# Three of the expert slots of a fused attention and mixture kernel hold 64 tokens, six slots run before routing is complete

## The chip, the cores and the metric

The kernel runs on one core of one Trainium2 chip. The metric is the device time of one execution in microseconds (us). It was timed in three runs; one more execution was recorded by the hardware profiler. The engines are named as in the profile: PE is the matrix engine (PEld its loading of weights), DVE the vector engine, ACT the scalar engine, POOL the general engine, SP the engine that issues most DMA transfers.

## The reference: linear attention, a gated dense layer, then a top-1 mixture of eight experts

```python
x = attention(q, k, v, omega)               # 4 x 576 = 2304 tokens of 512 features
x = rmsnorm(x) * g
x = (silu(x @ w_gate) * (x @ w_val)) @ w_out          # 512 -> 1536 -> 512
# the mixture ("MoE 2"): eight experts, each token goes to one
logits = x @ w_gate2 + modality_bias[modality_id]
e_idx = argmax(logits, axis=1)
gate_w = softmax(logits)[arange(N), e_idx]
for e in range(8):
    mask = e_idx == e
    h = maximum(x[mask] @ w1[e], 0.0)       # 512 -> 1024
    out[mask] = gate_w[mask, None] * (h @ w2[e])      # 1024 -> 512
```

With the inputs of this case the reference sends 873, 291, 576 and 564 tokens to four experts and none to the other four. The expert of token 0 is the one with 873, and all of its tokens lie among the first 2048.

## The kernel before

Tokens lie in 18 tiles of 128. Attention and the dense layer run woven into each other, two tiles (a chunk) at a time; the hidden products are at L1156, the products back at L1226, the routing logits at L1292. Every 32-bit number that goes into a product is parted into a high and a low 16-bit half, and a product takes three matmuls (high by low, high by high, low by high).

The mixture works in **slots** of 128 tokens of one expert. `slots` (L1835) loads for a slot the four parts of the expert's parted weights (`load`, L1842: four DMAs of 1 MB from `split_dram`, issued by SP, L1852) into a place of a ring of `RING` = 3, and `compute` (L1886) does the work: POOL gathers the rows of the slot's tokens by an indirect DMA (L1892), PE transposes them (L1881), ACT and DVE part them (L307 and L313, L317), PE does the first product (L1916: 96 matmuls with the weights held in the engine and 128 tokens as columns), ACT takes the maximum with zero (L1933), the result is parted again, PE does the second product (L1945: 24 matmuls with the tokens held and 512 features as columns), ACT or DVE scales the rows (L850, L854), and POOL scatters them into the output (L1973).

Which tokens a slot holds comes from tables. The first `NEARLY` = 4 slots all belong to the expert of token 0 (padded where that expert has fewer tokens); their tables are made from the first 16 tiles while the dense layer still works on the last two (`early_picks` to `early_indices`), and they share one load of weights. The tables of all other slots are made when the last two tiles have their logits: the rank products on PE (L1591, L1595), then one after the other on DVE `counts` (L1704), `late_places`, `late_values` (L1733), `experts` (L1777), with the table products on PE (L1763) when `late_values` is done, and `late_indices`. `slot_i` (L1793) holds each slot's expert and the number of slots; SP waits for it before it can issue the loads of the slots after the early ones. The first `NFIXED` = 20 slots always run. Where more are needed, branches behind them run the rest (`further`, L1997); here 7 + 3 + 5 + 5 = 20 are needed.

The order of the work is written out beforehand by a planner (`Plan`, L71): every step has a cost, the engines that may do it, and a time at which it is wanted (`want`); the planner plays the steps through and fixes each engine's order and which engine does a step that several may do. `NUDGES` (L49) shifts the wanted times of chosen ranges of steps. `spare` (L485) sets 140 matmuls of no use into stretches in which the planner finds PE idle (L491).

## Time and profile before

| | |
|---|---|
| median of three runs | 834.04 us (829.54 to 836.36) |
| the profiled execution, its own time | 831.05 us |
| its span in the profile | 829.3 us |
| PE busy | 811.4 us, 98% of the span |
| DVE busy | 542.6 us, 65% |
| ACT busy | 478.3 us, 58% |
| POOL busy | 293.6 us, 35% |
| mean granted clock of PE | 0.995 |

An engine is busy while one of its instructions runs; a matmul's time in the profile reaches from its start to its modelled end, and matmuls overlap, so the distance of two starts tells the rate, not the length of one.

### The profile page before, as it was taken

Reading aid. Unit: us, or ns where it says so; the run is one execution under the profiler, and the core shown is the slowest. Engines: PE = TensorE matmul, PEld = TensorE weight load, DVE = VectorE, ACT = ScalarE, POOL = GpSimd, SP = SyncE. Lnnn points to the kernel's source line nnn. Section 1 sums busy time; section 2 is a strip of 40 time slices with the busy share of each in tenths; the row PEclk is TensorE's granted clock in tenths of the full one; section 3 lists DMA queues with packets and bytes.
Section 4 is the critical chain, followed back from the end, with each engine's and each line's share of the span. In section 5 each row is a group of like instructions: output and inputs, shape, how many; then the busy total and the mean of one; then the engine's idle time right before and its main releaser. Section 6 shows DMA issues by size and latency. Waiting matters only on the chain. (4 is left out here: it accounts for less than half of the span.)

```text
span 829.3 us, 19951 instructions
## 1 busy us (share of the span) xinstructions
PE 811.4 (98%) x7900; PEld 632.7 (76%) x7900; DVE 542.6 (65%) x1262; ACT 478.3 (58%) x1132; POOL 293.6 (35%) x425
## 2 busy tenths in 40 slices
PE   9999989999999999999999999999999999999995
PEld 8899878887656778887777777777777777777773
DVE  5788988997647888888889989777673111222220
ACT  4767667778525888767878877664333233223321
POOL 0288898574222224232314344222202111222211
PEclk9999999999999999999999999999999999999998
DMA  8525441337204578756677676855418999999980
GB/s 269 186 78 204 132 138 63 111 128 285 67 27 132 178 238 278 245 171 211 218 236 238 225 218 217 283 199 211 172 40 331 423 421 425 423 426 424 424 357 21
DMA packets 38579, 188.06 MB, mean 227 GB/s; under 512 B 5071, under 2 KB 5199, under 8 KB 21584
## 3 DMA queue, kind: packets, MB, share of 16 engines
q1 hardware_dynamic: 35280, 176.72, 59.1%
q0 software_dynamic: 3200, 10.01, 3.2%
q8 instruction: 64, 1.05, 0.5%
q14 instruction: 35, 0.29, 0.1%
HBM read 143.68 MB, written 43.55 MB: 226 GB/s over the span
## 5 line engine op out<-in xcount | busy, mean ns | idle before, releaser
L1156 PE MATMUL bank<-x,big 128*128 128x256 f16 x2592 | 310.7, 273 | 2.0 <-DVE plain L1180 1.6
L1156 PEld LDWEIGHTS <-big 128*128 128x128 f16 x2592 | 250.7, 98 | 49.4 <-issue 2.9
L1226 PE MATMUL bank<-big 128*128 128x512 f16 x648 | 160.2, 379 | 0.0
L317 POOL TENSOR_TENSOR big<-plain,big 128x256 f16<-128x256 f32 x101 | 80.2, 796 | 182.4 <-ACT big L307 143.6
L1916 PEld LDWEIGHTS <-big 128*128 128x128 f16 x1920 | 111.8, 98 | 12.0 <-issue 0.2
L1916 PE MATMUL bank<-plain,big 128*128 128x128 f16 x1920 | 116.4, 219 | 0.0
L1945 PE MATMUL bank<-big,plain 128*128 128x512 f16 x480 | 115.0, 379 | 0.0
L844 DVE SCALAR_TENSOR_TENSOR big<-big,e_fac 128x512 f16<-128x512 f32 x128 | 102.4, 806 | 8.2 <-ACT big L850 7.3
L1226 PEld LDWEIGHTS <-big 128*128 128x128 f16 x648 | 61.3, 99 | 49.6
L317 DVE TENSOR_TENSOR plain<-plain 128x512 f16<-128x512 f32 (+1 forms) x44 | 30.5, 696 | 95.9 <-ACT plain L307 67.9
L1175 ACT ACTIVATE plain<-bank,w_scale 128x256 f32<-128x256 f32 x108 | 51.0, 472 | 57.7 <-PE bank L1156 45.7
L1065 ACT ACTIVATE plain<-big,plain 128x1024 bf16<-128x1024 f32 x64 | 73.5, 1149 | 12.4 <-DMA big<-in_w_exp_dram 12.0
L1945 PEld LDWEIGHTS <-plain 128*128 128x128 f16 x480 | 44.7, 98 | 40.3
L560 ACT ACTIVATE plain<-bank,plain 128x128 f32<-128x128 f32 x216 | 60.7, 376 | 19.4 <-DVE plain L554 19.4
L850 ACT ACTIVATE big<-big,e_fac 128x512 f16<-128x512 f32 x97 | 68.6, 716 | 1.6 <-DMA split_dram<-big 1.6
L1933 ACT ACTIVATE plain<-bank 128x512 f32<-128x512 f32 x40 | 23.8, 595 | 77.3 <-PE bank L1916 71.8
L1180 DVE SCALAR_TENSOR_TENSOR plain<-plain,bank 128x256 f32<-128x256 f32 x108 | 44.7, 415 | 27.2 <-ACT plain L1175 20.2
L554 DVE TENSOR_REDUCE plain<-bank 128x4 f32<-128x512 f32 x72 | 47.7, 683 | 19.7 <-PE bank L537 12.8
L307 ACT CAST big<-plain 128x256 f16<-128x256 f32 x94 | 37.7, 403 | 34.7 <-DVE plain L1202 18.0
L1960 POOL TENSOR_TENSOR plain<-plain,x 128x1 f32<-128x1 f32 x16 | 6.0, 374 | 126.9 <-DVE plain L854 82.2
L1194 POOL TENSOR_TENSOR plain<-plain,big 128x256 f32<-128x256 f32 x34 | 34.5, 1017 | 15.2 <-DVE plain L1180 12.1
L317 DVE TENSOR_TENSOR plain<-bank,plain 128x512 f16<-128x512 f32 (+1 forms) x38 | 26.2, 688 | 18.2 <-ACT plain L307 15.7
(261 smaller groups left out, 1138.6 us busy)
## 6 DMA issues: line engine op xcount, KB each, us to landing
big<-split_dram SPq DMA_DIRECT2D x68, 1024.0 KB, 19.4
big<-in_w_exp_dram SPq DMA_DIRECT2D x32, 1024.0 KB, 6.6
split_dram<-big SPq DMA_DIRECT2D x32, 1024.0 KB, 9.3
big<-in_w_moe_dram SPq DMA_DIRECT2D x36, 512.0 KB, 5.1
plain<-in_v_dram SPq DMA_DIRECT2D x18, 260.0 KB, 3.6
x_dram<-plain SPq DMA_DIRECT2D x18, 258.0 KB, 3.8
plain<-in_kT_dram SPq DMA_DIRECT2D x16, 256.0 KB, 2.5
plain<-in_qT_dram SPq DMA_DIRECT2D x16, 256.0 KB, 5.2
```

The costliest lines, as they stand in the source:

```text
L317: eng.tensor_tensor(out=out, in0=src, in1=hi, op=ALU.subtract)
L554: lambda: nc.vector.tensor_reduce(out=mx.tile, in_=pp.tile, axis=AX.X, op=ALU.min),
L560: nc.scalar.activation(ph[:, h, :], pp[:, h, :], AF.Exp, bias=mx[:, h : h + 1], scale=-1.0)
L844: nc.vector.scalar_tensor_tensor(out=out, in0=src, scalar=factor, in1=hi, op0=ALU.mult, op1=ALU.subtract)
L850: nc.scalar.activation(out, src, AF.Copy, scale=factor)
L1065: lambda c=c, h=h, cs=cs: nc.scalar.activation(junk.tile, raws[c][:, cs], AF.Square, bias=tiny, accum_out=sums[:, 2 * c + h : 2 * c + h + ...
L1156: nc.tensor.matmul(gv[:, t, :], w[a][:, kk, :], self.x[x][:, kk, :], start=kk == 0 and m == 0, stop=kk == KD - 1 and m == 2,)
L1175: lambda: nc.scalar.activation(th.tile, gv[:, 0, :], AF.Tanh, scale=one(BACK)),
L1180: lambda: nc.vector.scalar_tensor_tensor(out=th.tile, in0=th.tile, scalar=1.0, in1=gv[:, 0, :], op0=ALU.add, op1=ALU.mult,),
L1226: nc.tensor.matmul(self.acc[j].tile, h[:, a, r], out_w[f][:, i, :], start=f == 0 and m == 0, stop=f == FT - 1 and m == 2,)
L1916: nc.tensor.matmul(ph[:, j, :], w_of(c, p, k * F2 + (4 * n + j) * P, P), x[a][:, kk, :], start=kk == 0 and j == 0 and m == 0, stop=kk == K ...
L1945: nc.tensor.matmul(y.tile, hs[n][a][:, kk, :], w_of(2 + n, p, kk * DM, DM), start=f == 0 and m == 0, stop=f == KF2 - 1 and m == 2,)
```

## The change

Six slots are early instead of four, and share one load. Of the slots that always run, 17 hold 128 tokens and three hold 64; after the sixth to the last full slot in order, the three small ones stand behind the second, the fifth and the eighth of the eleven late full slots. The ring has four places. `counts` counts for each expert full slots and at most one small one (for a rest of up to 64 tokens), `experts` and `late_values` map slots and tokens accordingly, and `experts` now stands ahead of `late_values`. A small slot is `compute_half`: both products hold the weights in PE and have 64 tokens as columns (96 matmuls each); the second product therefore comes out with features by rows, and four more transposes turn it back. With the counts above, the slots are 7 + 2 + 4 + 4 = 17 full and 3 small ones (rests of 35, 64 and 52 tokens), so that nothing is left for the branches. The early tables' values are made by four DVE instructions instead of sixteen, and `NUDGES` has other numbers, and 26 instead of 18 of them.

```diff
-NEARLY = 4
-RING = 3
+NEARLY = 6
+NFULL = 17
+NHALF = 3
+RING = 4
...
-    (924, 2709, 7.5, 59), (316, 556, 2.75, 9), (125, 795, 4, 37), (263, 294, -4.75),
...
+    (924, 2709, 7.5, 59), (312, 540, 8.5, 9), (120, 792, 4.75, 37), (622, 675, -15, 34),
...
     def early_values():
-        for n in range(NEARLY):
-            nc.vector.tensor_scalar(mine.tile, loc[:, :TE], float(n), None, ALU.is_equal)
-            nc.vector.tensor_tensor(out=mine.tile, in0=mine.tile, in1=hot[:, :TE, 0], op=ALU.mult)
-            nc.vector.tensor_scalar(val_e[:, :, n, 0], mine.tile, it_p.tile, None, ALU.mult)
-            nc.vector.tensor_tensor(
-                out=val_e[:, :, n, 1], in0=mine.tile, in1=it_i[:, :TE], op=ALU.mult
...
+        shape = [P, TE, NEARLY]
+        nc.vector.tensor_tensor(
+            out=mine.tile,
+            in0=loc[:, :TE].unsqueeze(2).to_broadcast(shape),
+            in1=it_s[:, :NEARLY].unsqueeze(1).to_broadcast(shape),
+            op=ALU.is_equal,
+        )
+        nc.vector.tensor_tensor(
+            out=mine.tile, in0=mine.tile, in1=hot[:, :TE, 0:1].to_broadcast(shape), op=ALU.mult
+        )
+        nc.vector.tensor_scalar(val_e[:, :, :, 0], mine.tile, it_p.tile, None, ALU.mult)
+        nc.vector.tensor_tensor(
+            out=val_e[:, :, :, 1], in0=mine.tile,
+            in1=it_i[:, :TE].unsqueeze(2).to_broadcast(shape), op=ALU.mult,
+        )
+
...
     def counts():
-        tek = [P, E, NTILE]
-        nc.vector.tensor_copy(cnt.tile, rank[:, NTILE, :])
-        nc.vector.tensor_tensor(out=cnt[:, 0:1], in0=cnt[:, 0:1], in1=pad.tile, op=ALU.add)
+
+        tek = [P, 2 * E, NTILE]
+        over = past.tile.rearrange("p s e -> p (s e)")[:, : 2 * E * NTILE]
+        over = over.rearrange("p (e i) -> p e i", i=NTILE)
+        nc.vector.tensor_copy(cnt[:, 1, :], rank[:, NTILE, :])
+        nc.vector.tensor_tensor(out=cnt[:, 1, 0:1], in0=cnt[:, 1, 0:1], in1=pad.tile, op=ALU.add)
+        nc.vector.tensor_scalar(cnt[:, 0, :], cnt[:, 1, :], -float(Q), None, ALU.add)
...
-        nc.vector.tensor_reduce(out=n_slot.tile, in_=over.tile, axis=AX.X, op=ALU.add)
+        nc.vector.tensor_reduce(out=n_slot.tile, in_=over, axis=AX.X, op=ALU.add)
+        nc.vector.tensor_tensor(
+            out=n_slot[:, E:], in0=n_slot[:, E:], in1=n_slot[:, :E], op=ALU.subtract
+        )
         nc.vector.tensor_tensor_scan(end_e.tile, ones_f.tile, n_slot.tile, 0.0, ALU.mult, ALU.add)
         nc.vector.tensor_tensor(out=base_e.tile, in0=end_e.tile, in1=n_slot.tile, op=ALU.subtract)
+        full, more = end_e[:, E - 1 : E], many[:, 0:1]
+        nc.vector.tensor_scalar(more, full, -float(NFULL), 0.0, ALU.add, ALU.max)
...
+    def experts():
+
+        tse = [P, NSLOT, E]
+        full, last, more = end_e[:, E - 1 : E], end_e[:, 2 * E - 1 :], many[:, 0:1]
+        nc.vector.scalar_tensor_tensor(
+            out=s_at.tile, in0=it_o.tile, scalar=more, in1=it_s.tile, op0=ALU.mult, op1=ALU.add
+        )
+        nc.vector.tensor_scalar(s_at.tile, s_at.tile, full, -float(NFULL), ALU.add, ALU.add)
+        nc.vector.tensor_tensor(out=s_cl.tile, in0=it_q.tile, in1=s_at.tile, op=ALU.subtract)
+        nc.vector.scalar_tensor_tensor(
+            out=s_cl.tile, in0=it_q.tile, scalar=full, in1=s_cl.tile, op0=ALU.is_lt, op1=ALU.mult
+        )
+        nc.vector.tensor_tensor(out=s_at.tile, in0=s_at.tile, in1=s_cl.tile, op=ALU.add)
+        nc.vector.tensor_scalar(many[:, 1:2], last, -1.0, None, ALU.add)
+        nc.vector.tensor_scalar(s_at.tile, s_at.tile, 0.0, many[:, 1:2], ALU.max, ALU.min)
+        nc.vector.tensor_tensor(
+            out=past.tile,
+            in0=s_at.tile.unsqueeze(2).to_broadcast([P, NSLOT, 2 * E]),
+            in1=end_e.tile.unsqueeze(1).to_broadcast([P, NSLOT, 2 * E]),
+            op=ALU.is_ge,
+        )
+        ex = slot_f[:, :NSLOT]
+        nc.vector.tensor_reduce(out=ex, in_=past.tile, axis=AX.X, op=ALU.add)
+        nc.vector.tensor_scalar(s_cl.tile, ex, float(E), -float(E), ALU.is_ge, ALU.mult)
+        nc.vector.tensor_tensor(out=ex, in0=ex, in1=s_cl.tile, op=ALU.add)
+        nc.vector.tensor_scalar(ex, ex, e0[:, 0:1], None, ALU.add)
+        nc.vector.tensor_scalar(s_cl.tile, ex, 0.0, float(E), ALU.is_lt, ALU.mult)
+        nc.vector.tensor_tensor(out=ex, in0=ex, in1=s_cl.tile, op=ALU.add)
...
+        nc.vector.tensor_scalar(
+            many[:, 2:3], many[:, 2:3], 0.0, float(NFIXED), ALU.max, ALU.add
+        )
+        nc.vector.tensor_tensor(
+            out=slot_f[:, NSLOT:], in0=many[:, 2:3], in1=more, op=ALU.add
+        )
+        nc.vector.tensor_copy(slot_i.tile, slot_f.tile)
...
+    dve(
+        4.0, now, experts, reads=[end_e, it_s, it_q, it_o, e0, it_x, e_back],
+        writes=[many, s_cl, s_at, past, slot_f, slot_i, sc_s],
...
     def late_values():
+
         tie, tis = [P, NTILE, E], [P, NTILE, NSLOT]
-        nc.vector.tensor_tensor(
-            out=cand.tile, in0=hot.tile, in1=base_e.tile.unsqueeze(1).to_broadcast(tie), op=ALU.mult
-        )
-        nc.vector.tensor_reduce(out=slot.tile, in_=cand.tile, axis=AX.X, op=ALU.add)
+        col, more = many[:, 3:4], many[:, 0:1]
+
+        def of_token(out, per_expert):
+            nc.vector.tensor_tensor(
+                out=cand.tile, in0=hot.tile, in1=per_expert.unsqueeze(1).to_broadcast(tie),
+                op=ALU.mult,
+            )
+            nc.vector.tensor_reduce(out=out, in_=cand.tile, axis=AX.X, op=ALU.add)
+
+        nc.vector.tensor_scalar(
+            lots_of.tile, base_e[:, E:], end_e[:, E - 1 : E], None, ALU.subtract
+        )
+        nc.vector.tensor_scalar(cnt[:, 0, :], lots_of.tile, float(NHALF), more, ALU.is_ge, ALU.mult)
+        nc.vector.scalar_tensor_tensor(
+            out=lots_of.tile, in0=lots_of.tile, scalar=float(NFULL), in1=cnt[:, 0, :],
+            op0=ALU.add, op1=ALU.add,
+        )
+        of_token(slot.tile, n_slot[:, :E])
+        nc.vector.tensor_tensor(out=at_half.tile, in0=loc.tile, in1=slot.tile, op=ALU.is_ge)
+        of_token(slot.tile, base_e[:, :E])
+        nc.vector.tensor_tensor(out=loc.tile, in0=loc.tile, in1=slot.tile, op=ALU.add)
+        nc.vector.tensor_scalar(
+            slot.tile, loc.tile, float(NFULL), float(NHALF), ALU.is_ge, ALU.mult
+        )
+        nc.vector.tensor_tensor(out=loc.tile, in0=loc.tile, in1=slot.tile, op=ALU.add)
+        of_token(slot.tile, lots_of.tile)
+        nc.vector.tensor_tensor(out=slot.tile, in0=slot.tile, in1=loc.tile, op=ALU.subtract)
+        nc.vector.tensor_tensor(out=slot.tile, in0=slot.tile, in1=at_half.tile, op=ALU.mult)
...
-        def load(s, want):
-
-            place = 0 if s == 0 else (s - NEARLY + 1) % RING
+        def load(s, turn, want):
+
+            place = turn % RING
...
-        def transposed(src, want):
-            pt = buf("t", [P, 4, P], F32)
+        def transposed(src, want, rows=P):
+            pt = buf("t", [P, 4, rows], F32)
 
             def transposes():
                 for kk in range(4):
-                    nc.tensor.transpose(pt[:, kk, :], src[:, kk * P : (kk + 1) * P], ident)
-
-            plan.op("pe", 0.43, want, transposes, reads=[src], writes=[pt])
+                    nc.tensor.transpose(
+                        pt[:, kk, :], src[:rows, kk * P : (kk + 1) * P], ident[:rows, :rows]
+                    )
+
+            plan.op("pe", 0.43 if rows == P else 0.25, want, transposes, reads=[src], writes=[pt])
...
+        def compute_half(s, want):
+
+
+            xg = gather(idx, s, Q, want, False)
+            x = parted(transposed(xg, want - 5, Q), ("xgh", "xgl"), want - 20, Q)
+            w = weights[s]
+
+            def w_of(c, p, lo):
+                return w[c][:, p * 2048 + lo : p * 2048 + lo + P]
+
+            ph = buf("gv", [P, 2, 4, Q], F32)
+
+            def up(c):
+                for j in range(KF2):
+                    for k in range(KH):
+                        kk = c * KH + k
+                        for m, (a, p) in enumerate(((0, 1), (0, 0), (1, 0))):
+                            nc.tensor.matmul(
+                                ph[:, j // 4, j % 4, :], w_of(c, p, k * F2 + j * P),
+                                x[a][:, kk, :],
+                                start=kk == 0 and j == 0 and m == 0,
+                                stop=kk == KD - 1 and j == KF2 - 1 and m == 2,
+                                skip_group_check=True,
+                            )
+
+            for c in range(2):
+                plan.op(
+                    "pe", 1.42, want + 2 * c, lambda c=c: up(c), reads=[*x, w[c]], writes=[ph]
+                )
+            hs = []
+            for n in range(2):
+                hr = buf("hr", [P, 4, Q], F32)
+                plan.op(
+                    "act", 0.4, want - 20,
+                    lambda hr=hr, n=n: nc.scalar.activation(
+                        hr.tile, ph[:, n], AF.Relu, scale=2.0**-15
+                    ),
+                    reads=[ph], writes=[hr],
+                )
+                hs.append(parted(hr, ("hTh", "hTl"), want - 20, Q))
+            yT = buf("o", [P, KD, Q], F32)
+
+            def down(n):
+                for kk in range(4):
+                    for d in range(KD):
+                        for m, (a, p) in enumerate(((0, 1), (0, 0), (1, 0))):
+                            nc.tensor.matmul(
+                                yT[:, d, :], w_of(2 + n, p, kk * DM + d * P), hs[n][a][:, kk, :],
+                                start=n + kk + d + m == 0,
+                                stop=n == 1 and kk == 3 and d == KD - 1 and m == 2,
+                                skip_group_check=True,
+                            )
+
+            for n in range(2):
+                plan.op(
+                    "pe", 1.42, want + 4 + n, lambda n=n: down(n), reads=[*hs[n], w[2 + n]],
+                    writes=[yT],
+                )
+            ys, y = buf("hr", [P, KD, Q], F32), buf("t", [P, DM], F32)
+            plan.op(
+                {"act": 0.4, "dve": 0.42}, None, want - 10, lambda e: copy_on(e, ys.tile, yT.tile),
+                reads=[yT], writes=[ys],
+            )
+
+            def transposes():
+                for d in range(KD):
+                    nc.tensor.transpose(y[:Q, d * P : (d + 1) * P], ys[:, d, :], ident)
+
+            plan.op("pe", 0.43, want + 6, transposes, reads=[ys], writes=[y])
+            scatter(y, xg, idx, s, sc_s, s, Q, want)
...
-        for n, s in enumerate(which):
-            want = start + FT * n
+            scatter(y, xg, ix, col, *((sc_e, 0) if early else (sc_s, s)), P, want)
+
+        turn = 0
+        for s in which:
+            half = NFULL <= s < NFIXED
             if s == 0 or s >= NEARLY:
-                load(s, want - 24)
-            compute(s, want)
-
-    slots(plan, range(NFIXED), FT * NCH, True)
+                load(s, turn, start - 24)
+                turn += 1
+            (compute_half if half else compute)(s, start)
+            start += 0.55 * FT if half else FT
+
+    def in_order():
+        yield from range(NEARLY)
+        later, done = NFULL - NEARLY, 0
+        for n in range(later):
+            yield NEARLY + n
+            if done < NHALF and n % (later // NHALF) == 1:
+                yield NFULL + done
+                done += 1
+
+    slots(plan, list(in_order()), FT * NCH)
     plan.run()
 
     n_slots = nc.values_load(
-        slot_i[0:1, NSLOT : NSLOT + 1], min_val=NTILE, max_val=NSLOT
+        slot_i[0:1, NSLOT : NSLOT + 1], min_val=NFIXED, max_val=NSLOT
     )
```

The order of the instructions moves with it. On PE, in the part of the program with the late slots, this is where one late slot follows another before (L1945 the second product of one slot, L1881 the transposes of a later slot's tokens, L1916 the first product):

```order
L1945 LDWEIGHTS plain
L1945 MATMUL bank_96<-big,plain 128x512
L1881 MATMUL bank_89<-ident,plain 128x128 x4
...
L1916 LDWEIGHTS big
L1916 MATMUL bank_91<-plain,big 128x128
```

And this is the end of the first small slot now (L2057 its second product, L2077 the four transposes that turn it back, L2103 and L2132 the products of full slots around it):

```order
L2132 MATMUL bank_95<-big,plain 128x512
L2057 LDWEIGHTS big
L2057 MATMUL bank_96<-plain,big 128x64
...
L2103 LDWEIGHTS big
L2103 MATMUL bank_92<-plain,big 128x128
...
L2077 MATMUL bank_89<-ident,plain 64x128 x4
L2103 LDWEIGHTS big
L2103 MATMUL bank_94<-plain,big 128x128
```

Between the last matmul of the small slot's second product and the transposes stand the 24 matmuls of a full slot's first product. On DVE, where the late tables are made, the rows before run from the end of `late_values` through `experts` (`x_514` is the memory of the late tables, L317 the low half of an early slot's numbers, L1793 `slot_i`):

```order
L1749 TENSOR_SCALAR x_514<-x_514,xs 128x18x29
L1750 TENSOR_TENSOR x_514<-x_514,xs 128x18x29
L317 TENSOR_TENSOR plain<-bank_89,plain 128x512
L1779 TENSOR_SCALAR x_514<-x_514 128x1
L1780 TENSOR_SCALAR x_514<-xs,x_514 128x29
L1781 TENSOR_TENSOR x_514<-x_514 128x232
...
L1793 CAST x_514<-x_514 128x30
```

Now the end of `experts` (L1798 is `slot_i`) runs into `late_values` (from L1841), with one low half (L321) between them:

```order
L1798 CAST x_514<-x_514 128x32
L1800 TENSOR_TENSOR x_514<-x_514,xs 128x31x8
L1806 TENSOR_TENSOR x_514<-x_514,xs 128x31x8
L1809 TENSOR_REDUCE x_514<-x_514 128x31
L321 TENSOR_TENSOR plain<-plain 128x512
L1841 TENSOR_SCALAR x_514<-x_514 128x8
L1844 TENSOR_SCALAR x_514<-x_514 128x8
```

The table products on PE, which read what `late_values` writes, now have `experts` ahead of them on DVE. Between the rank products and the table products PE has 36 matmuls of 512 columns, 120 of 128 and four transposes now. Up to the beginning of the third chunk's hidden products PE's order is the same as before; from there to the end of the dense layer steps stand in another order on every engine.

## Rows read from the trace of the kernel before

**Rows 1.** The page's first two parts: PE in all; DMA in 40 slices.
```profile
PE 811.4 (98%) x7900; PEld 632.7 (76%) x7900; DVE 542.6 (65%) x1262; ACT 478.3 (58%) x1132; POOL 293.6 (35%) x425
...
DMA  8525441337204578756677676855418999999980
```
**Rows 2.** Busy time by stretch: us, PE, PEld, DVE, ACT, POOL, clock, DMA, GB/s.
```profile
150.00:200.00 50.00, 47.83 (x473) 41.38 (x471) 46.41 (x92) 36.68 (x102) 29.34 (x36) 1.00 0.51 173
...
660.00:680.00 20.00, 19.95 (x230) 15.00 (x229) 4.81 (x7) 5.89 (x10) 4.75 (x6) 1.00 1.01 423
```
**Rows 3.** What PE waited for, whole span: us in total, times, longest.
```profile
PE bank L1156 <- DVE plain L1180: 1.6, 4, 0.7
PE bank L1134 <- POOL plain L823: 1.3, 1, 1.3
```
**Rows 4.** PE in order of time, two late slots: start, us, instructions.
```profile
771.12 0.60 PE L1881 MATMUL bank<-ident,plain 128*128 128x128 f32 x4
...
771.56 1.46 PE L1945 MATMUL bank<-big,plain 128*128 128x512 f16 x6
...
774.59 1.50 PE L1916 MATMUL bank<-plain,big 128*128 128x128 f16 x24
775.93 1.46 PE L1945 MATMUL bank<-big,plain 128*128 128x512 f16 x6
777.22 5.52 PE L1916 MATMUL bank<-plain,big 128*128 128x128 f16 x96
...
793.08 0.60 PE L1881 MATMUL bank<-ident,plain 128*128 128x128 f32 x4
```
**Rows 5.** PE in order of time, narrow products of the attention.
```profile
491.71 0.53 PE L759 MATMUL bank<-plain 128*128 128x65 f16 x12
492.08 0.36 PE L1081 MATMUL bank<-plain,ones_w 128*128 128x1 f32 x2
```
**Rows 6.** PE in order of time, rank and table products and what follows.
```profile
614.26 0.17 PE L1591 MATMUL bank<-xs 128*128 128x8 bf16 x1
...
622.70 0.28 PE L1763 MATMUL bank<-x,xs 128*128 128x58 bf16 x4
...
623.21 1.46 PE L1945 MATMUL bank<-big,plain 128*128 128x512 f16 x6
```
**Rows 7.** Groups by form: busy us, mean ns of one, idle before.
```profile
L759 PE MATMUL bank<-plain 128*128 128x65 f16 x264 | 11.8, 193 | 1.1 <-DVE plain L1180 0.8 <-DVE plain L593 0.3
L1916 PEld LDWEIGHTS <-big 128*128 128x128 f16 x1920 | 111.8, 98 | 12.0 <-issue 0.2
```
**Rows 8.** DMA from 620 us on: queue (packets, MB, share); loads (KB, us to landing).
```profile
q0 software_dynamic: 2800, 8.69, 10.4%
...
big<-split_dram SPq DMA_DIRECT2D x64, 1024.0 KB, 19.4
```
**Rows 9.** SP in order of time: the loads of the late slots.
```profile
624.44 167.87 SPq L1852 DMA_DIRECT2D big<-split_dram  x64
```
**Rows 10.** DVE in order of time: the late tables.
```profile
614.65 0.16 DVE L1706 COPY x<-bank 128x8 f32<-128x8 f32 x1
...
616.01 0.17 DVE L1612 TENSOR_TENSOR xs<-bank,xs 128x16 f32<-128x16 f32 x1
...
617.62 0.68 DVE L317 TENSOR_TENSOR plain<-plain 128x512 f16<-128x512 f32 x1
618.22 0.30 DVE L1738 TENSOR_TENSOR xs<-xs,x 128x144 f32<-128x144 bf16 x1
...
620.73 0.69 DVE L317 TENSOR_TENSOR plain<-bank,plain 128x512 f16<-128x512 f32 x1
621.33 0.14 DVE L1779 TENSOR_SCALAR x<-x 128x1 f32<-128x1 f32 x1
...
624.62 0.21 DVE L1815 COPY x<-bank 128x58 f32<-128x58 f32 x1
```
**Rows 11.** The end: PE's last products, the last scatter.
```profile
816.87 2.75 PE L1945 MATMUL bank<-big,plain 128*128 128x512 f16 x12
...
820.67 0.98 POOL L1973 DMA_INDIRECT out_dram<-plain,x  x1 [4.36 <-ACT plain L850]
```

186 lines of the change are left out of this document (93 added, 93 removed), and 9 rows, old and new, of the table NUDGES.

## The prediction

> **What bounds the kernel now.** I read the page's shares first: PE is busy for 98% of the span, every other engine for at most two thirds [rows 1]. A busy PE may still run below its rate, so the second view is PE in order of time. Among the late slots 24 narrow matmuls take 1.34 us (774.59 to 775.93), 55.8 ns each, six wide ones 1.29 us (775.93 to 777.22), 215 ns each, four transposes 0.44 us (771.12 to 771.56), 109 ns each; a slot has four groups of 24, four of six and one of four, 4 x (1.34 + 1.29) + 0.44 = 10.96 us [rows 4]. The transposes of one slot and of the slot two later start 21.96 us apart, 10.98 us a slot [rows 4]: the slots run at PE's own rate with nothing between them. Third, the waits. In a stretch of 20 us of late slots PE lacks 0.05 us at the full clock [rows 2], and the longest waits of the whole list come to 1.6 and 1.3 us [rows 3]. So the program is as long as PE's work, and a step leaves the time if it leaves PE.
>
> One other resource is at its edge: DMA is busy for the whole stretch of late slots, 1.01 of it at 423 GB/s [rows 1, 2]. A late slot needs 4 x 1.05 MB of weights and, by 35 indirect transfers with 8.69 MB [rows 8], two of 0.25 MB: 4.69 MB, which at 423 GB/s takes 11.1 us, as long as PE's 10.98. That PE doesn't wait means that the loads keep just ahead. A PE that gets faster alone would run into them.
>
> **The change part by part.** *Three small slots instead of three full ones.* Each takes 10.98 us from PE and puts back 2 x 96 matmuls of 64 columns with fresh weights for each, four transposes of 64 rows and four transposes back. What does such a matmul take? The trace has two rows beside it. Twelve attention products of 65 columns take 0.37 us (491.71 to 492.08), 30.8 ns each [rows 5]; there are 264 of this form with their own weights [rows 7]. The eighteen table products of 58 columns take 0.51 us (622.70 to 623.21), 28.3 ns [rows 6]. 64 columns lie between the two; I take 30 ns, so 192 x 30 = 5.76 us. The transposes of 64 rows take between half of 0.44 us and all of it, I take 0.3; those back have full columns, 0.44. Together 6.5 us, a gain of 4.48 us a slot and **13.4 us for three**. The ends: at 28.3 ns and 0.22 us the slot takes 6.1 us and the gain is 14.6 us; the upper end is the rival below.
>
> The trace shows such narrow matmuls in runs of at most 18, the small slot brings runs of 48. Its loading of weights lasts 98 ns [rows 7] while its matmul starts every 55.8 ns [rows 4], so loads overlap already, by two at a time; at 30 ns more than three must. The eighteen show that this holds for half a microsecond. The Trainium skill speaks against this term: the page "TensorE: Matmul & The Clock Gate", section "Back-to-back issue gap", gives pairs of weight load and matmul a sustained 81 ns at 128 columns and sets the plain quotient of columns and clock below that, since the load of weights has its share. If 64 columns cost the same as 128 by that rule, a small slot would take 192 x 81 ns and 0.74 us, an estimate of 16.3 us, and the kernel would be 16 us slower. The trace doesn't agree: its sustained pairs of 128 columns stand at 55.8 ns [rows 4].
>
> Inside a small slot the second product can start when ACT has taken the maximum and ACT and DVE have parted the numbers, three steps of at most 0.7 us; between them PE has two groups of 24 and one of six of full slots (4 us). The copy ahead of the transposes back is covered by 24 matmuls (1.34 us) alone, one step of ACT or DVE of about half the size of 0.7 us: cost nothing, and if that cover failed some tenths of a us, three times.
>
> *Six early slots and a ring of four places.* These move no work on PE: six times 128 rows of the same expert, which has 873 tokens, are full. They take loads away: 14 late slots are loaded instead of 16, 56 DMAs instead of the 64 that SP issues from 624.4 us on [rows 9]. The loads' need: 14 x 4.19 MB and at most 8.69 MB of rows [rows 8] are 67.4 MB, at 423 GB/s 159 us, so they could be through at 783 us. PE reaches the first late slot two slots later, about 22 us, and by then three loads (3 x 11.1 us) are in place. From there three full slots and a small one take PE 3 x 10.98 + 6.5 = 39.4 us and DMA 4 x 9.9 us of weights and 4 us of rows, 44 us: PE gains 4.6 us on the loads in each of three such rounds, 14 us, against a lead of about 33. I take no cost; with the ring of three and four early slots the lead would have been gone in the second round.
>
> *The late tables.* On DVE `counts` took 1.36 us (614.65 to 616.01), `late_places` 1.61, a low half 0.60, `late_values` 2.51 (618.22 to 620.73), and after another low half `experts` 3.29 us (621.33 to 624.62, twelve instructions, 0.27 us each) [rows 10]. The table products on PE started 8.4 us after the rank products (614.26 to 622.70) [rows 6], and their values were ready at 620.7, so nobody waited. Now `counts` has three instructions more and two of twice the width (2.25 us by 0.2 us a small one), `late_places` is as before, `experts` has 21 instead of 12 and two of twice the width (3.29 + 1.8 + 0.6 = 5.7), a low half 0.6, and `late_values` 19 instead of 6 (2.51 + 13 x 0.22 = 5.4). With the 0.39 us from the rank products to the first of them that is 15.9 us. PE has between the two products, by its new order, 36 wide and 120 narrow matmuls and four transposes: 36 x 0.215 + 120 x 0.0558 + 0.44 + 0.1 = 15.0 us. So **PE waits about 0.9 us** at the table products, 0 to 3 by the error of the small instructions. Behind the wait stand the second products of early slots. `slot_i`, which opens the loads, now stands ahead of `late_values`: some 9 us after the rank products, as before (624.44 less 614.26 is 10.2 [rows 6, 9]). The early tables lose twelve DVE instructions in a place where PE has dense-layer work: nothing.
>
> *The new `NUDGES`.* From the beginning of the third chunk, some 150 us into the span, to the end of the dense layer every engine's order is another one. What it could still gain is small, since PE's idle in these stretches is: 2.2 us from 150 to 200 us [rows 2], with single waits under a us after that. What it could lose is not bounded so: DVE is busy 46.4 of 50 us there [rows 2], and a badly placed step makes PE wait. I take +0.5 us, with -2 and +6 for the range.
>
> *The end.* The last slot is a full one as before; from PE's last products (816.87 + 2.75 = 819.6) and the scatter at 820.7 [rows 11] to the end of the span (829.3) nothing changes.
>
> **The sum:** 831.05 - 13.4 + 0.9 + 0.5 = 819.0 us against the profiled execution's own time. That execution lies 3.0 us below the median of the three timed runs (834.04) and inside their spread; the timed median should come out between 819 and 822, and I put it at **820 us**.
>
> **The rivals.** *Narrow products cost like their weights.* If in runs of 48 the loading of weights doesn't keep up, the price of a pair rises towards what rows show for wider ones. With 55.8 ns [rows 4] a small slot takes 10.7 + 0.74 = 11.45 us and the three cost 1.4 us more: 834 us, no change. With the whole 98 ns of a load [rows 7] it takes 19.6 us, and the kernel would end at 834 + 26 = 860 us. It turns from a gain to a loss at (10.98 - 0.74) / 192 = 53 ns. For it: no run longer than 18 in the trace. Against: 264 pairs of one form at about 30 ns [rows 5, 7]. I give 10% in all, 4% of it for a price above 53 ns; the skill's 81 ns would be within these 4%.
>
> *The new order of the middle makes PE wait.* DVE's near-full stretch loses its slack and PE waits for L1180 or the parted inputs. At 6 to 12 us lost the time is 826 to 832; it would take more than 15 us, seven times the idle time that 150 to 200 us shows, to be slower than before. Against it: the waits listed so far are short though DVE was as full. 12% for 6 us or more, 3% of it for slower.
>
> *The loads become the bound.* If a place comes free late or the first loads start late, the lead of 33 us shrinks and PE is paced by 11.1 us a load. The worst is that the 14 us are not gained: 833 us. It takes a start of the loads some 19 us later than 624 us, or a ring place that waits for something outside the slots. 6%.
>
> *The change does not do what it says:* were one more token in an expert's rest than its small slot takes, a branch would run one slot more with nothing to cover it. The counts (rests of 35, 64 and 52) fit, one of them exactly, so 1%.
>
> **The chances.** My own case, 812 to 826 us, has 71%. About 1% is what a measurement of this kernel can tell from no change (8.3 us). The range of 812 to 829 us holds the forecast with the bounds of its terms (14.6 gained and -2 from the order at one end, the 6 us of the order with 3 us of waits at the other) and the smaller half of the second rival; outside stay the price of a full weight load and the loads as the bound. Faster by over 1%, that is below about 825.5: 0.74; within 1%: 0.18, from the rivals at 834 and the upper part of the order's range; slower: 0.08, from the price above 53 ns, the lost order, and the extra branch.
>
> **What the profile will show.** Right: the groups of 48 matmuls of 64 columns take 1.4 to 1.5 us each from first start to the next group's; DMA falls below full in the late slots now and then, SP issues 60 loads in all instead of 68; the late full slots still take 10.98 us of PE; PE's only new wait in the last 230 us is one of about 1 us at the table products, for DVE; PE ends about 13 us earlier. Wrong: groups of 48 at 2 us or more; PE waiting for `big<-split_dram`; or a list of PE's waits between 150 and 600 us that adds up to much more than 3 us.

## The result and the profile after

The changed kernel took 836.42 us (median of 20 runs, 832.20 to 843.43) against 831.94 for the kernel before (20 runs): a ratio of 1.0053, 95% interval 1.0033 to 1.0073. It did not become faster by 14 us, as predicted, but slower by 4. Its profiled execution took 835.43 us, with a span of 833.7.

The first part of the page of the changed kernel, PE's line:

```profile
PE 805.1 (97%) x8128; PEld 631.3 (76%) x8128; DVE 548.6 (66%) x1290; ACT 470.4 (56%) x1122; POOL 296.6 (36%) x427
```

PE is busy for 6.3 us less than before [rows 1], and yet the span is 4.4 us longer. What PE lost must be idle time, or work at a lower clock. The list of PE's waits in the changed kernel (us in total, times, longest) names the first:

```profile
PE bank L1962 <- DVE plain L858: 11.6, 2, 5.9
PE bank L1881 <- DVE x L1868: 1.7, 1, 1.7
```

Before, no line of that list came to more than 1.6 us [rows 3]. Now the transposes of gathered tokens (L1962, L1881 before) wait twice for the scaling of rows (L858, L854 before), 5.7 and 5.9 us. The windows of the late slots show where (us, PE, PEld, DVE, ACT, POOL, clock, DMA, GB/s):

```profile
680.00:700.00 20.00, 20.00 (x358) 16.57 (x356) 4.69 (x8) 5.53 (x12) 5.14 (x6) 1.00 1.01 413
700.00:720.00 20.00, 14.28 (x128) 10.18 (x126) 4.02 (x6) 3.43 (x6) 2.49 (x3) 0.83 0.90 362
720.00:740.00 20.00, 20.00 (x300) 15.99 (x299) 4.87 (x9) 6.58 (x12) 5.58 (x7) 1.00 0.90 356
740.00:760.00 20.00, 14.14 (x205) 11.61 (x203) 4.03 (x7) 3.90 (x7) 3.84 (x6) 0.83 1.01 409
```

Two of the four stretches lack 5.7 and 5.9 us of PE, and in the same two the granted clock is 0.83; a late stretch before had 19.95 us at the full clock [rows 2]. The chain of waits around the first of them, in order of time (start, us, what):

```profile
698.41 7.70 DMA out_dram<-plain,x
...
706.23 0.75 DVE plain L858
...
707.03 1.11 PE bank L1962 x4
708.15 2.56 PE bank L2103 x24
```

This is read from the bottom up. PE's transposes waited for the scaling of the small slot's rows on DVE, and that waited for a DMA: the scatter of the full slot ahead, issued at 698.41, landed only 7.70 us later. DVE's own row says the same, with its idle time and what ended it behind; ahead of it the row of PE's transposes that turn the small slot's rows back:

```profile
699.37 0.60 PE L2077 MATMUL bank<-ident,plain 128*64 128x128 f32 x4
...
706.23 0.74 DVE L858 TENSOR_SCALAR plain<-bank,plain 64x512 f32<-64x512 f32 x1 [9.82 <-DMA out_dram<-plain,x]
```

PE had turned the rows back by 699.8 (699.37 and the 0.44 us of four transposes). In the 6.4 us from there on the scaling had nothing to wait for but its place to write to; the first 3.4 of the 9.82 us are not the scatter's. Then PE runs on at half the rate for a while: 24 matmuls of 128 columns take 2.56 us instead of 1.34 [rows 4]. The second occurrence on PE, in order of time:

```profile
747.26 0.60 PE L2077 MATMUL bank<-ident,plain 128*64 128x128 f32 x4
747.70 1.50 PE L2103 MATMUL bank<-plain,big 128*128 128x128 f16 x24
755.06 1.11 PE L1962 MATMUL bank<-ident,plain 128*128 128x128 f32 x4 [5.86 <-DVE plain L858]
755.97 2.77 PE L2103 MATMUL bank<-plain,big 128*128 128x128 f16 x24
758.52 1.72 PE L2132 MATMUL bank<-big,plain 128*128 128x512 f16 x4
```

It cost 5.86 us of idling, and at the low clock 0.91 - 0.44 us in the transposes, 2.55 - 1.34 in the 24 matmuls and about 0.8 in the next four wide ones: 2.5 us more, 8.4 us in all. Twice that is 16.8 us, and the profiled execution lies 835.43 - 819.0 = 16.4 us above my sum. Ahead of the scaling of the third small slot DVE is idle too, for 4.88 us. But the scatter ahead, issued at 795.52, has landed by 799.92, 4.4 us later, while the last loads run out. The slot's rows are turned back only by 799.6 (its transposes start at 799.18), so this landing costs some 0.3 us at most, and PE does not wait:

```profile
799.92 0.74 DVE L858 TENSOR_SCALAR plain<-bank,plain 64x512 f32<-64x512 f32 x1 [4.88 <-DMA out_dram<-plain,x]
```

The view of the scatters' output tells who waited for them; ahead of the change it told it too, and I had not read it. Of the kernel before, then of the changed one:

```profile
who waited for it (us, times):
  ACT plain L850: 27.1, 6
...
DMA to landing us min/median/max: 2.9/6.7/7.6
```

```profile
who waited for it (us, times):
  DVE plain L858: 32.1, 4
...
DMA to landing us min/median/max: 2.8/5.5/8.6
```

So scalings stood behind scatters before as well, six times, and PE did not feel it. The 27.1 us are idle time of ACT that a landing ended; how much of it the landing itself cost, the second experiment shows.

My theory after this reading: the scaled rows (`yo`) have two places in memory, but the planner gives every slot the first, since by its own account a scatter lets go of its source when POOL has issued it. The rows of a small slot are ready some 1.4 us after the scatter of the slot ahead is issued (698.41 to 699.8), long before it lands, so their scaling waits; and its turned-back rows stand in the bank of PE that the next transposes need (`t`), so that PE waits as well. The rivals were the loads, the new order of the middle, and a ring or early slots that cost something themselves.

### The profile page after: what moved, and what is told of

It reads as the page before. It is cut to its first block, busy times and chain, and to the rows that moved or that the text cites. A ratio compares the mean times of both kernels' runs of the same rounds, so it can differ in the third digit from the quotient of the medians.

```text
span 833.7 us, 20364 instructions
## 1 busy us (share of the span) xinstructions
PE 805.1 (97%) x8128; PEld 631.3 (76%) x8128; DVE 548.6 (66%) x1290; ACT 470.4 (56%) x1122; POOL 296.6 (36%) x427
## 4 chain that ended last, share of the span: by engine, by line
PE 73%; DVE 9%; issue 7%; POOL 5%; DMA 4%; ACT 1%; POOLq 0%; DVEq 0%; ACTq 0%
PE bank L1160 25%; PE bank L1230 17%; PE bank L2103 7%; PE bank L2132 6%; PE bank L613 4%; PE bank L541 4%; DMA out_dram<-plain,x 4%; PE bank L495 2%; PE bank L763 2%; POOL plain L1198 2%; PE bank L579 2%; DVE big L876 1%; PE bank L1962 1%; PE bank L1269 1%; POOL big L321 1%
## 5 line engine op out<-in xcount | busy, mean ns | idle before, releaser
L1160 PEld LDWEIGHTS <-big 128*128 128x128 f16 x2592 | 250.3, 98 | 47.8 <-issue 2.0
L321 POOL TENSOR_TENSOR big<-plain,big 128x256 f16<-128x256 f32 x98 | 78.9, 807 | 160.4 <-ACT big L311 109.0
L848 DVE SCALAR_TENSOR_TENSOR big<-big,e_fac 128x512 f16<-128x512 f32 x128 | 105.8, 840 | 4.7 <-ACT big L854 3.9
L2103 PEld LDWEIGHTS <-big 128*128 128x128 f16 x1632 | 98.1, 99 | 9.8 <-issue 0.7
L2103 PE MATMUL bank<-plain,big 128*128 128x128 f16 x1632 | 103.6, 222 | 0.4 <-ACT plain L2120 0.4
L1230 PEld LDWEIGHTS <-big 128*128 128x128 f16 x648 | 62.4, 100 | 51.9 <-issue 2.2
L2132 PE MATMUL bank<-big,plain 128*128 128x512 f16 x408 | 98.1, 383 | 0.0
L564 ACT ACTIVATE plain<-bank,plain 128x128 f32<-128x128 f32 x216 | 60.7, 376 | 16.4 <-DVE plain L558 16.3
L854 ACT ACTIVATE big<-big,e_fac 128x512 f16<-128x512 f32 x98 | 68.0, 719 | 1.0 <-DMA split_dram<-big 0.7
L2132 PEld LDWEIGHTS <-plain 128*128 128x128 f16 x408 | 38.2, 99 | 37.7 <-issue 1.9
L2120 ACT ACTIVATE plain<-bank 128x512 f32<-128x512 f32 x34 | 20.2, 598 | 73.3 <-PE bank L2103 72.7
L321 DVE TENSOR_TENSOR plain<-plain 128x512 f16<-128x512 f32 (+3 forms) x43 | 27.9, 657 | 48.6 <-ACT plain L311 48.6
L311 ACT CAST big<-plain 128x256 f16<-128x256 f32 x87 | 34.9, 403 | 34.6 <-DVE plain L1206 18.9
L321 DVE TENSOR_TENSOR plain<-bank,plain 128x512 f32<-128x512 f32 (+2 forms) x38 | 25.2, 666 | 32.0 <-ACT plain L311 31.7
L858 DVE TENSOR_SCALAR plain<-bank,plain 128x512 f32<-128x512 f32 (+1 forms) x10 | 7.5, 747 | 56.2 <-DMA out_dram<-plain,x 24.7
```

The lines of the kernel that those rows point to most:

```text
L321: eng.tensor_tensor(out=out, in0=src, in1=hi, op=ALU.subtract)
L564: nc.scalar.activation(ph[:, h, :], pp[:, h, :], AF.Exp, bias=mx[:, h : h + 1], scale=-1.0)
L848: nc.vector.scalar_tensor_tensor(out=out, in0=src, scalar=factor, in1=hi, op0=ALU.mult, op1=ALU.subtract)
L854: nc.scalar.activation(out, src, AF.Copy, scale=factor)
L1160: nc.tensor.matmul(gv[:, t, :], w[a][:, kk, :], self.x[x][:, kk, :], start=kk == 0 and m == 0, stop=kk == KD - 1 and m == 2,)
L1230: nc.tensor.matmul(self.acc[j].tile, h[:, a, r], out_w[f][:, i, :], start=f == 0 and m == 0, stop=f == FT - 1 and m == 2,)
```

## The experiments

**Places in turn, in the changed kernel.** Every engine keeps its instructions in the same order; only the place of `yo` alternates.

```diff
+        def one_of(name, shape, dt):
+            n = count[name] = count.get(name, -1) + 1
+            places = areas[name]
+            return Buf([places[n % len(places)]], shape, dt, queues.setdefault(name, []))
...
-            yo, fac = buf("yo", [P, DM], F32), buf("fac", [P, 1], F32)
+            yo, fac = one_of("yo", [P, DM], F32), buf("fac", [P, 1], F32)
```

> The changed kernel with one thing changed: the scaled rows of one slot after the other (yo) take the two places of that buffer in turn, where the planner gave every slot the first one; no instruction moves on any engine. Theory (one place): in the changed kernel the scaling of a small slot's rows waits until the scatter of the slot before has landed (698.4 to 706.1 us, 7.7 us), and since the rows to be scaled stand in a bank that the next transposes need, PE waits 5.9 us, twice, and then runs at half its clock for some 2.5 us: 8.4 us each. With the places in turn both waits go, and the time is 835.4 - 16.8 = 818.6 us. Rival (order of the scatters): the scaling waits because scatters into the same output are kept in order, whatever the place; then both waits stay and the time is that of the changed kernel, 835 us.

Measured: 820.64 us (817.69 to 824.77), ratio to the kernel before 0.9853 (0.9818 to 0.9887). The wait at the transposes is gone, and the two windows are full at the full clock:

```profile
700.00:720.00 20.00, 20.00 (x246) 15.55 (x243) 5.65 (x9) 5.92 (x10) 5.98 (x8) 1.00 1.01 422
740.00:760.00 20.00, 20.00 (x240) 15.44 (x238) 5.55 (x9) 5.40 (x10) 5.72 (x7) 1.00 1.01 424
```

One buffer's place is worth 16 us here, and without that fault the change gives what was predicted of it.

The rival is not wholly gone. In time order around the first small slot:

```profile
700.40 1.01 POOL L2007 DMA_INDIRECT out_dram<-plain,x  x1 [0.58 <-issue]
...
702.06 0.74 DVE L858 TENSOR_SCALAR plain<-bank,plain 64x512 f32<-64x512 f32 x1 [3.66 <-PE bank L2084]
...
708.74 0.94 POOL L2007 DMA_INDIRECT out_dram<-plain,x  x1 [5.16 <-DMA out_dram<-plain,x]
```

The scaling now starts 1.7 us after the scatter ahead is issued, but the small slot's own scatter still starts only when that one has landed. POOL stands idle for 22.8 us in four such waits. So scatters are kept in order here; that holds up POOL and not the scaling, and PE does not feel it.

**The same in the kernel before.** The same edit of `yo` there.

> The kernel before with the same one thing: the places of yo in turn. There the scaling of every second late slot also waited for the scatter before it (six waits of 4.4 to 4.8 us on ACT), but the rows stand in one of two banks for second products, and PE did not wait. Theory (one place): the waits of ACT go, PE does what it did, the time stays within 1 us of the kernel before. Rival (order of the scatters): the waits of ACT stay, same time. A gain of more than 3 us would mean that the waits cost something before too.

Measured: 831.22 us, 0.9991 (0.9968 to 1.0014). ACT no longer waits for a scatter, and nothing is won: the wait was there, and hidden. It was also shorter than ACT's idle time. The scaling of a late slot in the kernel before, then the same one here behind the scatter ahead of it:

```profile
690.64 0.69 ACT L850 ACTIVATE plain<-bank,plain 128x512 f32<-128x512 f32 x1 [4.40 <-DMA out_dram<-plain,x]
```

```profile
683.99 1.02 POOL L1980 DMA_INDIRECT out_dram<-plain,x  x1 [0.20 <-issue]
...
689.77 0.69 ACT L850 ACTIVATE plain<-bank,plain 128x512 f32<-128x512 f32 x1 [3.40 <-PE bank L1952]
```

Without the wait ACT is still idle for 3.40 us, until PE has finished the rows, so the scatter cost about 1 us of the 4.40. The scaling comes 5.8 us behind the issue of the scatter ahead, and that scatter lands after 6.7 us in the median; behind a small slot it is 1.7 us, as the first experiment shows.

**Only the planner's figure for the scatter.**

```diff
-                reads=[yo, ix], lag=2.0,
+                reads=[yo, ix], lag=8.0,
```

> The changed kernel with one number changed: the planner is told that a scatter's source is free 8.0 us after its issue, instead of 2.0. No instruction moves on any engine. Theory (the planner gave every slot the first place because it took the place to be free after 2 us, while a scatter lands after 7.7 us beside the loads): with 8.0 it gives two slots that follow closely two places, the two waits of 5.9 us go, and the time is that of the run with the places in turn, 820 us. Rival (the turns of the places helped by something else than this figure): the waits stay and the time is 836 us.

Measured: 836.30 us, 1.0046 (1.0020 to 1.0072), with PE's list unchanged (11.6 us in two at the transposes). A detail of my theory fell: `lag` delays the users of a step's result only, and the planner sets a step's buffers free when its cost (1.3 us) is over, whatever the lag.

**The planner holds a scatter's source until it lands.** The corrected theory, tried in the planner itself.

```diff
-                heapq.heappush(events, (busy[e], -1, None) if e == "dma" else (busy[e], best.n, best))
-                if e == "dma":
+                best.held = e == "dma" or best.lag == 8.5
+                heapq.heappush(events, (busy[e], -1, None) if best.held else (busy[e], best.n, best))
+                if best.held:
...
-                reads=[yo, ix], lag=2.0,
+                reads=[yo, ix], lag=8.5,
```

> The changed kernel with the planner taught that a scatter holds its source until it lands (8.5 us after it is issued) and not only for the 1.3 us in which its engine issues it. Nothing else is changed: every engine has the instructions of the changed kernel in the same order. My theory, corrected after the run with the longer lag alone: the planner gave the scaled rows the first of their two places each time because by its own bookkeeping that place was free again after 1.3 us. Then the planner now picks the places in turn by itself, the scaling no longer waits for a scatter, PE's three waits of 11.6 us for the scaling go, and the time is that of the kernel with places in turn: 820.6 us, 818 to 823. Rival: taking the places in turn by hand did something else as well (another place in memory, another set of semaphores), or the order of the scatters on their queue is what holds the rows; then the waits stay wholly or in part and the time lies between 828 and 836 us.

Measured: 816.42 us (815.95 to 818.68), 0.9815 (0.9799 to 0.9832). The instructions stand in the changed kernel's order, the places alternate, and the waits for the scaling (two, where the expectation says three) are gone. Its median lies below the 818 to 823 expected. The two kernels were timed on different chips, and the intervals of their ratios overlap. The profiled execution of the one with places in turn was 3.9 us behind the other after the first 45 us, long before the slots, and 2.2 us at the end. The windows of the two from 20 to 40 us, places in turn first (columns as above), tell where that comes from:

```profile
20.00:40.00 20.00, 20.00 (x167) 17.99 (x167) 12.88 (x22) 13.06 (x46) 1.64 (x4) 0.74 0.58 195
```

```profile
20.00:40.00 20.00, 20.00 (x214) 18.22 (x213) 15.71 (x29) 17.32 (x60) 4.07 (x7) 1.00 0.62 209
```

I take them for one time. This is the fastest version, and both beat the two kernels given.

**The turned-back rows in another bank.** The changed kernel with its one place for `yo`, and the rows of a small slot in a bank of the second products, which the next transposes don't use.

```diff
-            ys, y = buf("hr", [P, KD, Q], F32), buf("t", [P, DM], F32)
+            ys, y = buf("hr", [P, KD, Q], F32), buf("o", [P, DM], F32)
```

> The changed kernel, with one place of yo as it is, but the transposes back of a small slot write into a bank of the second products (o) instead of one of the transposes (t). PE's order is the same; the next matmuls that need that bank now stand four transposes and 24 matmuls further on (0.44 + 1.34 us). Theory (the late scatter holds up the scaling, the scaling holds the bank, the bank holds PE): DVE still waits for the scatter, but PE waits at second products of full slots instead of at transposes, and some 1.8 us less each: twice 4.1 instead of 5.9 us, and 832 to 833 us in all. Rival (the bank is not the link; PE waits for something else that DVE does): waits of 5.9 us as in the changed kernel, 836 us.

Measured: 830.65 us, 0.9979 (0.9952 to 1.0005), some 2 us below what was expected. PE's list now has this at its head:

```profile
PE bank L2132 <- DVE plain L858: 7.9, 2, 4.1
```

The wait for the scaling moved from the next transposes to the next second product, 4 us instead of 5.8. So the bank is the link through which DVE's wait reaches PE, and moving it only shortens the wait; the place of `yo` ends it. A second link stands right behind the first. The same second product needs a low half (L321) that DVE makes only after the scaling, and PE's weight loads wait for it (the first matmul had started at 704.40):

```profile
704.27 0.67 DVE L321 TENSOR_TENSOR plain<-plain 128x512 f16<-128x512 f32 x1
...
705.00 0.56 PEld L2132 LDWEIGHTS <-plain 128*128 128x128 f16 x4 [0.50 <-DVE plain L321]
```

So a bank that nobody else needs would not have freed PE either.

**Four early slots and the ring of three, with places in turn.** `NEARLY` 4 and `RING` 3 in the first experiment's kernel.

> The changed kernel with the places of yo in turn, and with four early slots and a ring of three places as before: the small slots alone. The prediction says that three full slots and a small one take PE 39.4 us and the loads 44 us, so that without the longer lead PE has to wait for loads: the 16 late loads with their rows need 16 x 11.1 = 178 us from 624.4 us on, the last is there at about 802 us and PE ends some 8 us later, at 810 against 806 without waits. Theory (loads): PE waits for big<-split_dram, 4 to 10 us in all, and the time is 822 to 829 us. Rival (loads are still hidden): no such waits, and the time is that of the run with the places in turn within 1 us.

Measured: 827.76 us (822.79 to 828.73), 0.9918 (0.9886 to 0.9951), with PE waiting for loads and gathers:

```profile
PE bank L2110 <- DMA big<-split_dram: 5.4, 5, 2.7
...
PE bank L1969 <- DMA plain<-x_dram,x: 1.5, 2, 0.8
```

Small slots on PE need the loads that the six early slots and the fourth place save; the two together are worth 7 us.

**The old `NUDGES`, with places in turn.** The numbers of before in the first experiment's kernel.

> The changed kernel with the places of yo in turn, and with the NUDGES of the kernel before: up to the end of the dense layer PE's order is that of before. The prediction put +0.5 us (-2 to +6) on the new numbers. By the trace of the changed kernel PE waits no longer between 150 and 600 us than before (its list of waits there adds up to less than 2 us). Theory (nudges are worth little): within 2 us of the run with the places in turn. Rival (the new order costs or gains there): 3 us or more away from it, with the difference between 150 and 600 us.

Measured: 822.03 us (819.74 to 825.89), 0.9871 (0.9835 to 0.9906). The new numbers are worth 1.4 us or nothing: the two intervals overlap.

**`late_values` ahead of `experts`, with places in turn.** The two DVE steps in the order of before.

> The changed kernel with the places of yo in turn, and late_values ahead of experts again, as in the kernel before. The one wait left in the run with the places in turn is 1.7 us of PE at the table products for the last instruction of late_values. Theory: the values are ready some 5 us sooner, the wait goes, the loads start some 5 us later and are still hidden by the longer lead; 1.7 us less than the run with the places in turn, 819 us. Rival (something else is late next: the loads, or the low halves of early slots behind the tables on DVE): the wait moves to another place and the time stays 820 to 821 us.

Measured: 821.20 us, 0.9848 (0.9817 to 0.9879). No gain. The wait at the table products fell from 1.7 to 0.4 us, and a new one stands behind it:

```profile
PE bank L1969 <- DVE plain L321: 2.1, 1, 2.1
...
PE bank L1881 <- DVE x L1864: 0.4, 1, 0.4
```

DVE has the same work in either order, and it's the low halves of early slots that come late now, as the rival had it.

**Six early slots and a ring of four in the kernel before.** Only these two numbers, with 20 full slots.

> The kernel before with six early slots and a ring of four places, all 20 slots full: this part of the change alone. The prediction says that it moves no work on PE and only takes loads away, so no gain: PE's own rate set the late slots before. Theory (PE-bound): 832 us as before, within 2 us, with DMA no longer full all the time and loads that land sooner after their issue than 19 us. Rival (the loads held PE back before in a way that a busy PE hides): 3 us or more faster.

Measured: 840.53 us (836.52 to 843.06), 1.0093 (1.0061 to 1.0125). Slower, which neither side had expected. PE in order of time where it lost most:

```profile
627.43 1.50 PE L1916 MATMUL bank<-plain,big 128*128 128x128 f16 x24
631.81 0.66 PE L1881 MATMUL bank<-ident,plain 128*128 128x128 f32 x4 [2.88 <-DMA plain<-x_dram,plain]
632.30 2.12 PE L1916 MATMUL bank<-plain,big 128*128 128x128 f16 x24
634.22 2.55 PE L1945 MATMUL bank<-big,plain 128*128 128x512 f16 x6
636.60 1.50 PE L1916 MATMUL bank<-plain,big 128*128 128x128 f16 x24
```

and POOL there:

```profile
620.46 0.19 POOL L1960 TENSOR_TENSOR plain<-plain,xs 128x1 f32<-128x1 f32 x1 [18.03 <-ACT plain L850]
621.26 1.53 POOL L1973 DMA_INDIRECT out_dram<-plain  x1 [0.61 <-PE bank L1881]
623.10 0.98 POOL L1892 DMA_INDIRECT plain<-x_dram,plain  x1 [0.30 <-issue]
```

On POOL the gather of the fifth early slot (the third, by mistake, in the two expectations below) is queued behind the factors of the third (L1960), which wait for the scaling of the first, and behind the first one's scatter; it is issued at 623.10, when DMA is already full of the late slots' loads, and PE waits for its rows until 631.81: 2.9 us of idling and 1.7 us (1.92 - 1.34 and 2.38 - 1.30) at the low clock.

**The ring alone, and the six early slots alone,** in the kernel before: `RING` 4, and `NEARLY` 6.

> The kernel before with a ring of four places for weights in place of three, and nothing else. It is one half of the run with six early slots and a ring of four, which came out 8.3 us slower than the kernel before. My theory: those 8 us come from the six early slots (the third of them stood for 2.9 us at its gathered rows, with 1.8 us more at half the clock, at 632 us; the rest in waits below 1.3 us), and the ring costs nothing: 832 us, 830 to 834, with PE's list of waits as before. Rival: the fourth place takes memory that other buffers of the late stage had, or lets the loads crowd the gathers and scatters; then 836 us or more, with new waits of PE from 640 us on.

> The kernel before with six early slots in place of four and the ring of three as it was, and nothing else: the other half. My theory: the third early slot's gather comes late as it did with the ring of four, so PE waits about 3 us at the transposes of its rows around 632 us, and loses about 2 us more there at half the clock; with the small waits that is 840 us, 837 to 842. Rival: the loss needed both (six early slots with four places, since loads and gathers share the transfers); then 831 to 835 us.

Measured: the ring alone 831.65 us, 1.0021 (0.9984 to 1.0059), no change; the six early slots alone 840.28 us, 1.0104 (1.0071 to 1.0137), with the same wait for gathered rows (3.0 us). So it is the early slots. With six early slots alone PE ends at 829.5 us against 819.6 in the kernel before. Some 5 us of that are lost in the 20 us around this gather, some 2 in the 20 us ahead of it; the rest is small losses elsewhere, not taken apart.

Why the changed kernel doesn't have this gather late, no run shows. With the old `NUDGES` it hasn't either, so these aren't it. A likely cause is a part of the change that its section leaves out: gathered rows have three places in memory instead of two, and the factors of rows four instead of two.

```diff
+    areas["xg"] += areas["seed"]
...
-    areas["fac"] = areas["ss"]
+    areas["fac"] = areas["ss"] + areas["se"]
```

In the changed kernel the fifth gather is issued at 597.35, long before the loads of the late slots, and not behind factors that wait for a scaling:

```profile
597.35 0.97 POOL L1973 DMA_INDIRECT plain<-x_dram,xs  x1 [1.18 <-PE bank L1269]
```

No run tries these places in the kernel before.

## Why the prediction was wrong

**The step that failed** is the one on the inside of a small slot: its copy and its turning back were costed by their cover on PE, "cost nothing, and if that cover failed some tenths of a us, three times". The end of the slot, scaling and scatter, wasn't costed at all; I took it as the full slot's. But it is what the change moves: it brings a scaling from 5.8 to 1.7 us behind the issue of the scatter ahead, of whose landing the trace said 6.7 us in the median and 7.6 at most, and it puts the rows into a bank with another user close behind. The price was 8.4 us twice.

The reading under it was "a step leaves the time if it leaves PE". I took the short list of PE's waits [rows 3] as proof that no other engine matters, and read no list of the others'. ACT's waits behind scatters, about 1 us each, were covered, since PE did not need their banks soon. The change makes such a wait 6.4 us long, in front of a bank that PE needs after 24 matmuls (1.34 us). None of my rivals had it, and neither did what I named as signs of being wrong.

**The small slots' price was right.** Narrow products in runs of 48, in the changed kernel:

```profile
794.81 0.46 PE L2057 MATMUL bank<-plain,big 128*128 128x64 f16 x10
...
796.44 1.56 PE L2057 MATMUL bank<-plain,big 128*128 128x64 f16 x48
797.84 1.50 PE L2103 MATMUL bank<-plain,big 128*128 128x128 f16 x24
```

From 796.44 to 797.84 are 1.40 us, 29.2 ns each, where I took 30 from the short runs [rows 5, 6]. The rival of the weights fell. The Trainium skill (page "TensorE: Matmul & The Clock Gate", section "Back-to-back issue gap") gives a sustained 81 ns for a pair of weight load and matmul at 128 columns; if 64 columns cost as much, 48 of them would take 3.9 us, an estimate from the page's figure. The trace doesn't agree, with its 1.40 us. With the places mended, the profiled executions take 821.09 us (places in turn by hand) and 818.68 us (by the planner) against the sum of 819.0. That the second lies within 0.4 us is luck: the two differ by more through the clock before the slots.

**The tables** were right in kind, and short in size: PE waits 1.7 us at the table products, where I had 0.9. From the rank products (610.32) to their values DVE took 16.8 us (15.9 in the sum), while PE's work between them was 15.0 as worked out:

```profile
624.04 1.46 PE L2132 MATMUL bank<-big,plain 128*128 128x512 f16 x6
627.17 0.25 PE L1881 MATMUL bank<-x,xs 128*128 128x62 bf16 x3 [1.68 <-DVE x L1868]
...
627.71 1.46 PE L2132 MATMUL bank<-big,plain 128*128 128x512 f16 x6
629.01 0.60 PE L1962 MATMUL bank<-ident,plain 128*128 128x128 f32 x4
```

**The loads** were right: PE waits for none, and without the six early slots and the fourth place it does. That six early slots cost nothing holds in the changed kernel alone; by themselves they cost the kernel before 8 us. **`NUDGES`** are worth about nothing, as taken. **The rivals** of the order and of the extra branch didn't occur: between 150 and 600 us the changed kernel's list of PE's waits has a single line, of 0.4 us.

## What to carry to other kernels

When a step becomes shorter, list what waits unseen behind the old length: for each buffer that a DMA reads, the time to its landing against the new distance to its next writer. An idle time that a landing ended is not all the landing's: of 4.4 us it was 1 here. A planner that counts a DMA's source as free when the DMA is issued hands out one place again and again while another lies idle. And a bank or buffer that joins a slow engine's result to the next piece of the fast engine's work is the way by which a hidden wait comes out.

## What the runs showed of the hardware

An idle PE costs more than its idle time. After 5.9 us of waiting it ran its next work at the lower of its two clock levels: 24 matmuls in 2.55 us instead of 1.34, the granted clock 0.83 over 20 us, 2.5 us lost on top. After the 2.9 us of the late gather 24 matmuls took 1.92 us and the next six wide ones 2.38 instead of 1.30, before the rate came back. After the 1.7 us at the table products nothing of the kind shows (six wide ones from 627.71 to 629.01, 1.30 us).

The clock can also be low in one execution and full in another at the same place of the program. From 20 to 40 us the granted clock was 0.74 in the profiled execution with places in turn and 1.00 in the one in which the planner holds the source, with the same list of PE's waits up to there (one, of 1.3 us). What makes the difference is open.

A scatter of at most 0.25 MB lands 7.7 us after its issue while DMA moves 360 to 410 GB/s, and within 4.4 us while the last loads run out; the shortest took 2.8 us.
